# Buffers rounded to 512 bytes, and four small pads that shift the weight buffers and some inputs against the others

## The chip, the cores and the metric

The program runs on one core of a Trainium2 chip. The metric is device time of one execution in microseconds (us). A core has a matrix engine (TensorE, PE in the tables, with PEld for its weight loads), a vector engine (VectorE, DVE), a scalar engine (ScalarE, ACT), GpSimd (POOL) and a queue engine (SyncE, SP). Operands lie in an on-chip memory of 128 partitions; every buffer below has the same start address in each partition. All addresses and sizes in this document are bytes within one partition.

## The reference

A block attention whose output feeds a gated linear unit, both in 32-bit floats:

```
scores = q @ k^T / sqrt(64)                 # 8 batches, 8 heads, 576 positions, 64 per head
heads 0-3: keep keys with 0 <= row - key < 32
heads 4-7: keep keys <= row in the same class modulo 32
attn   = softmax(scores) @ v
x      = attn, heads side by side           # 4608 tokens x 512
y      = (sigmoid(x @ w_gate) * (x @ w_val)) @ w_out     # 512 -> 1536 -> 512
```

Nearly all arithmetic is in the last line: three products with 512 x 1536 or 1536 x 512 matrices.

## The kernel before

Every float operand of the large products is split into a high part and a low remainder, and one product is done as three matmuls in the one-pass float format (fp32r): high x high, high x low, low x high. `three` issues them in this order for weights `wh, wl` and inputs `xh, xl`: (wh, xh), (wh, xl), (wl, xh). In each matmul a 128 x 128 block of the first operand is loaded into the engine as weights (one LDWEIGHTS), and 512 columns of the second stream through it (the moving operand).

The tokens are handled in a first part (the first batch, 512 tokens) and then four superblocks of up to two batches. The first part forms `g` and `v` (gate and value) from inputs named `x0_0` to `x0_3` (buffers `t0` to `t3`; the profile strips digits and prints `x`) and weights `w` (buffers `w0` to `w3`), then output sums `o`. In a superblock, two batches and two feature chunks are combined in a seven-product scheme (P1 to P7): inputs `x0` to `x6`, each with a high and a low part, and weights `mix` with seven parts of high and low. For five of the inputs, high and low are buffers of their own (`x0h`, `x0l`, ...); `x4` and `x5` are one buffer each with both halves, and the profile prints both as `x` (rows `x,mix`). Each of the seven products of one of the six pairs of chunks is 6 matmuls into a gate bank `g` and then 6 into a value bank `v`, in the order P1, P5, P6, P2, P7, P3, P4, whose inputs by the table `X_OF` are x0, x1, x3, x2, x5, x4, x6 (the very first pair alone does P2 ahead of P6).

The second half of superblocks 2 to 4 is the product with `w_out`, by parts as well; its operands share one buffer called `stage`: moving columns and weights lie in the same buffer. Superblock 1 does it plainly, with moving `wo` and weights `hs` in neighbouring buffers of the ring.

`mix`, `stage`, `wo` and `hs` all take the next of the ring of four buffers `w0` to `w3` in turn (`next_of_ring`). Between the large products stand short runs of small matmuls of the attention of later batches (scores `s`, transposes `t`, weighted values `x<-pt,vv`).

The order on every engine is written out by hand in the strings `ORDERS` and recorded as it stands (`manual_schedule`). Buffers come from one pool, `keep`: a tag gets its place when it is first asked for, directly behind the tag before it (rounded up to 32 bytes), and keeps it. So the sizes and the order of first requests fix every address. `flat` is the helper that asks for nearly all of them; `LINE = 32` floats (128 bytes) is its rounding.

Of the kernel before, what the change touches and what calls it, by code (L numbers as in the profile page):

```python
# [18 lines left out]
DM, DF = 512, 1536  # L19
NT = B * S  # L20
P = 128
LINE = 32
STRIDE = 32
QB = 64
LB = 32
# [223 lines left out]
def attention_then_glu(ctx, tc, qk_l, qk_s, v_l, v_s, w_all, consts, out):  # L249
    nc = tc.nc  # L250
    pool = ctx.enter_context(tc.tile_pool(name="keep", bufs=1))
# [4 lines left out]
    of_start = ExitStack()  # L256
    start_ps = of_start.enter_context(tc.tile_pool(name="start_ps", bufs=1, space=bass.MemoryType.PSUM))

    def flat(tag, n, name, dtype=F32):

        spare = -n % LINE
        return pool.tile([P, n + spare], dtype, tag=tag, name=name)[:, :n] if spare else pool.tile([P, n], dtype, tag=tag, name=name)

    cst = pool.tile([P, SL * KL + GS + P], F32, tag="cst", name="cst")
    some = slice(0, P), slice(P, P + SL * KL), slice(P + SL * KL, P + SL * KL + GS)
    ident, mask_l, mask_s = (cst[:, part] for part in some)
    mask_l = mask_l.rearrange("p (j n) -> p j n", j=1)
# [13 lines left out]
    def first_inputs():  # L281
        for c in range(NC):
            both = flat(f"t{c}", 2 * TB, f"x0_{c}", F32R)
            xs0["h", c], xs0["l", c] = both[:, :TB], both[:, TB:]
# [4 lines left out]
    def batch_tiles(b):  # L289
        if b not in rest:  # L290
            rest[b] = flat("xr", NC * REST, f"xr{b}")
            if b:
                raw[b] = flat("raw_a" if b % 2 else "raw_b", NC * TB, f"raw{b}")
# [1004 lines left out]
```

## Time and profile before

| | |
|---|---|
| median of 2 runs | 914.35 us (913.95 and 914.75) |
| the profiled execution's own time | 913.73 us |
| its span, first to last instruction | 911.9 us |
| PE busy, share of the span | 904.4 us, 99% |
| DVE, ACT, POOL busy | 615.3, 458.4, 288.2 us |
| granted TensorE clock over the span | 0.999 of full speed |
| chain of waits that ended last | PE 97%, DVE 2% |

The rounded shares of the page say that PE works all the time, but not how densely: a matmul's printed length is modelled and overlaps the next one's. The timeline is better for that: it prints the start of each merged run of matmuls and the count, so the distance between two starts divided by the count is the time that one matmul takes in the stream.

### The profile page before, as it was taken

What the parts mean: (1) busy time and instruction counts of PE and PEld (TensorE: products, weight loads), DVE (VectorE), ACT (ScalarE), POOL (GpSimd) and SP (SyncE); (2) the same over time, 40 slices, a digit from 0 to 9 for tenths busy, and PEclk for the clock granted to TensorE, in tenths of its full rate; (3) what the DMA queues carried; (4) which work ended last, traced back from release to release, by engine and by line L of the source; (5) the groups of instructions that cost most, each with busy time, mean ns of one, the idle gap of its engine ahead of it and who ended that gap; (6) DMA issues with size and microseconds to landing.
All of it is one profiled execution on the core that took longest, in us unless ns stands there. A gap on an engine that the chain in (4) does not pass through costs nothing.

```text
span 911.9 us, 18834 instructions
## 1 busy us (share of the span) xinstructions
PE 904.4 (99%) x7612; PEld 735.3 (81%) x7612; DVE 615.3 (67%) x967; ACT 458.4 (50%) x839; POOL 288.2 (32%) x234
## 2 busy tenths in 40 slices
PE   9999999999999999999999999999999999999997
PEld 8788888888888778888878888888888888888887
DVE  6887767887646788878678987322699853223955
ACT  5776887585433343646446544322546443233451
POOL 3244336644210252522025451000415620001165
PEclk9999999999999999999999999999999999999999
DMA  8888872865526789999664689558346796651566
GB/s 326 301 313 312 294 263 92 346 283 236 238 88 222 247 276 341 383 354 336 262 219 144 203 266 313 207 220 323 135 131 202 226 296 247 234 224 46 162 206 165
DMA packets 91623, 220.76 MB, mean 242 GB/s; under 512 B 35856, under 2 KB 50832, under 8 KB 84368
## 3 DMA queue, kind: packets, MB, share of 16 engines
q1 hardware_dynamic: 87216, 218.50, 67.7%
q10 hardware_dynamic: 4320, 1.05, 0.5%
q8 instruction: 60, 0.98, 0.4%
q14 instruction: 27, 0.22, 0.1%
HBM read 171.29 MB, written 48.23 MB: 241 GB/s over the span
## 4 chain that ended last, share of the span: by engine, by line
PE 97%; DVE 2%; issue 0%; ACT 0%; POOL 0%; DVEq 0%; POOLq 0%
PE g__2137 L610 15%; PE v__2139 L610 15%; PE v__2141 L610 10%; PE g__2140 L610 10%; PE g__2136 L610 10%; PE v__2138 L610 10%; PE x L471 4%; PE o L660 4%; PE g L610 3%; PE v L610 3%; PE s L368 3%; PE g__2140 L660 2%; PE v__2141 L660 2%; PE g__2136 L660 1%; PE v__2138 L660 1%; PE g__2137 L660 1%
## 5 line engine op out<-in xcount | busy, mean ns | idle before, releaser
L929 POOL TENSOR_TENSOR stage<-h,stage 128x512 fp32r<-128x512 f32 x50 | 75.5, 1529 | 165.9 <-ACT stage L927 144.7
L927 ACT CAST stage<-h 128x512 fp32r<-128x512 f32 x126 | 73.2, 620 | 73.6 <-issue 21.2
L443 DVE STREAM_TRANSPOSE pt<-sb 32x320 f32<-32x320 f32 (+1 forms) x160 | 85.8, 536 | 17.8 <-PE x L471 14.1
L796 DVE TENSOR_TENSOR s<-g__2137,gp 128x512 f32<-128x512 f32 x24 | 16.6, 690 | 79.1 <-PE g__2137 L610 58.5
L929 DVE TENSOR_TENSOR stage<-h,stage 128x512 fp32r<-128x512 f32 x76 | 61.7, 830 | 9.6 <-ACT stage L927 5.9
L798 ACT ACTIVATE s<-s 128x512 f32<-128x512 f32 x48 | 30.3, 633 | 54.7 <-DVE s L796 54.6
L797 DVE TENSOR_TENSOR h<-s 128x512 f32<-128x512 f32 x48 | 36.2, 761 | 23.6 <-ACT s L798 22.8
L798 ACT ACTIVATE s<-g__2137 128x512 f32<-128x512 f32 x24 | 14.3, 595 | 59.3 <-PE g__2137 L610 59.3
L610 PE MATMUL g__2137<-stage 128*128 128x512 f32 (+1 forms) x162 | 39.4, 380 | 0.0
L610 PE MATMUL v__2139<-stage 128*128 128x512 f32 (+1 forms) x162 | 39.3, 379 | 0.0
L610 PE MATMUL v__2141<-x,mix 128*128 128x512 f32 x144 | 37.7, 396 | 0.0
L610 PE MATMUL g__2140<-x,mix 128*128 128x512 f32 x144 | 37.7, 396 | 0.0
L610 PE MATMUL v__2139<-x,mix 128*128 128x512 f32 x144 | 37.6, 396 | 0.0
L610 PE MATMUL g__2137<-x,mix 128*128 128x512 f32 x144 | 37.5, 395 | 0.0
L847 POOL TENSOR_TENSOR hs<-h,hs 128x512 fp32r<-128x512 f32 x12 | 15.4, 1294 | 65.3 <-ACT hs L845 65.3
L471 PEld LDWEIGHTS x<-pt,vv 64*64 64x64 f32 (+1 forms) x1592 | 28.5, 134 | 8.9 <-issue 8.1
L610 PE MATMUL g<-x,w 128*128 128x512 f32 x132 | 34.1, 402 | 0.4 <-DVE x L506 0.4
L402 POOL TENSOR_TENSOR sb<-sb,mx 128x648 f32<-128x648 f32 (+1 forms) x9 | 12.8, 1420 | 68.4 <-DVE mx L394 68.2
L610 PE MATMUL v__2139<-x3h,mix 128*128 128x512 f32 x96 | 34.1, 395 | 0.0
L610 PE MATMUL v__2141<-x1h,mix 128*128 128x512 f32 x96 | 34.0, 395 | 0.0
L610 PE MATMUL g__2136<-x2h,mix 128*128 128x512 f32 x96 | 33.9, 394 | 0.0
L610 PE MATMUL g__2137<-x6h,mix 128*128 128x512 f32 x96 | 33.9, 394 | 0.0
(280 smaller groups left out, 2487.7 us busy)
## 6 DMA issues: line engine op xcount, KB each, us to landing
mix<-mix SPq DMA_DIRECT2D x36, 1024.0 KB, 8.8
mix<-mix SPq DMA_DIRECT2D x36, 768.0 KB, 6.5
mix<-mix SPq DMA_DIRECT2D x12, 1792.0 KB, 6.2
stage<-sums_out SPq DMA_DIRECT2D x72, 256.0 KB, 3.6
stage<-outer SPq DMA_DIRECT2D x54, 256.0 KB, 3.2
wo<-outer SPq DMA_DIRECT2D x8, 1536.0 KB, 6.8
vv<-in_v_l SPq DMA_DIRECT2D x16, 640.0 KB, 6.4
qk<-in_qk_l SPq DMA_DIRECT2D x16, 592.0 KB, 6.3
```

What stands on the lines that cost most here:

```text
L368: nc.tensor.matmul(sc[g * m : (g + 1) * m, j * BANK + s * kk : j * BANK + (s + 1) * kk], qk[d, q0 : q0 + m], qk[d, k0 : k0 + kk], start=no ...
L402: engine.tensor_tensor(prob, src, by_row, op=ALU.subtract)
L443: nc.vector.transpose(dst[to : to + LB, :, col : col + LB], src[rows : rows + LB, :, h * LB : (h + 1) * LB])
L471: nc.tensor.matmul(xp[j * D : (j + 1) * D, r * BANK + (u * per + g) * m : r * BANK + (u * per + g + 1) * m], v[rows, (u * per + g) * P + j ...
L610: nc.tensor.matmul(o, w, x, start=first and n == 0, stop=last and n == len(todo) - 1, skip_group_check=onto)
L660: nc.tensor.matmul(o, a[:, i * P : (i + 1) * P], b, start=first and n == 0, stop=last and n == 2)
L796: add = lambda to, x, y: nc.vector.tensor_tensor(to, x, y, op=ALU.add)
L797: mul = lambda to, x, y: nc.vector.tensor_tensor(to, x, y, op=ALU.mult)
L798: sig = lambda to, x: nc.scalar.activation(to, x, AF.Sigmoid)
L847: engine.tensor_tensor(hl, src, hh.bitcast(F32), op=ALU.subtract)
L927: nc.scalar.copy(h, src)
L929: engine.tensor_tensor(l, src, h.bitcast(F32), op=ALU.subtract)
```

## The change

`flat` now rounds a buffer to `ROW = 128` floats (512 bytes) if it has at least that many, and leaves smaller ones as they are. The two small buffers for row maxima (`mx`, `mx2`) are asked for first, right behind the constants. And at the first request of `w0`, `w1`, `w2` and `x6h`, a pad of 8, 8, 16 and 24 floats (32, 32, 64 and 96 bytes) is put ahead.

```
-LINE = 32
+ROW = 128
+APART = {'w0': 8, 'w1': 8, 'w2': 16, 'x6h': 24}
...
+    seen = set()
+
     def flat(tag, n, name, dtype=F32):

-        spare = -n % LINE
+        if tag in APART and tag not in seen:
+            pool.tile([P, APART[tag]], dtype, tag=tag + "_apart", name=tag + "_apart")
+        seen.add(tag)
+        spare = -n % ROW if n >= ROW else 0
...
+    for tag in ("mx", "mx2"):
+        flat(tag, 16, tag)
```

On each of the five engines the built program holds the same instructions in the same order with the same waits as before; only addresses differ. Start of each buffer modulo 256, from the built programs (before: modulo 512 in brackets):

| buffers, in the order of their addresses | before | after |
|---|---|---|
| t0 to t3 (x0_0 to x0_3 of the first part) | 96 (96) | 224 |
| x1h, x3h, x5, x4, x0l | 96 (352) | 224 |
| x0h | 224 (480) | 224 |
| w0 | 224 (480) | 0 |
| x1l, x2h, x3l | 224 (480) | 0 |
| w1 | 224 (480) | 32 |
| w2 | 224 (480) | 96 |
| x6h, x2l, x6l | 224 (480) | 192 |
| w3, and all that follow | 224 (480) | 192 |

Before, every one of these starts is 96 modulo 128. Within a buffer, weights begin at multiples of 512 bytes and moving operands of 512 columns at multiples of 2048, so these remainders hold for every large matmul. The last buffer ends 352 bytes later than before.

Below, the **distance** of a matmul is the difference between the start of its moving operand and the start of the weights that are loaded for the matmul behind it, modulo 256 and the shorter way round, so 0 to 128. Counted in program order over the 3455 matmuls of 512 columns that have another behind them (small matmuls between left out):

| matmuls of 512 columns | before: 0 / 128 | after: 0 / 32 / 64 / 96 / 128 |
|---|---|---|
| first part, g and v (288) | 0 / 288 | 0 / 148 / 70 / 0 / 70 |
| x4 and x5 with mix (576) | 0 / 576 | 0 / 288 / 144 / 0 / 144 |
| x0 with mix (288) | 192 / 96 | 0 / 144 / 72 / 0 / 72 |
| x1 and x3 with mix (576) | 192 / 384 | 48 / 240 / 144 / 48 / 96 |
| x2 with mix (288) | 288 / 0 | 72 / 48 / 72 / 96 / 0 |
| x6 with mix (288) | 288 / 0 | 72 / 0 / 72 / 144 / 0 |
| o of the first part (144) | 144 / 0 | 33 / 0 / 35 / 76 / 0 |
| wo with hs (288) | 288 / 0 | 0 / 140 / 8 / 140 / 0 |
| stage (719) | 719 / 0 | 660 / 15 / 29 / 15 / 0 |
| all (3455) | 2111 / 1344 | 885 / 1023 / 646 / 519 / 382 |

## Rows read from the trace of the kernel before

**Rows 1.** The page: the span, busy time by engine, the granted clock, the last chain.

```profile
span 911.9 us, 18834 instructions
...
PE 904.4 (99%) x7612; PEld 735.3 (81%) x7612; DVE 615.3 (67%) x967; ACT 458.4 (50%) x839; POOL 288.2 (32%) x234
...
PEclk9999999999999999999999999999999999999999
...
PE 97%; DVE 2%; issue 0%; ACT 0%; POOL 0%; DVEq 0%; POOLq 0%
```

**Rows 2.** Waits of PE: who waited for whom, us in total, times, longest.

```profile
PE zeros_out L651 <- POOL zeros L642: 1.0, 1, 1.0
PE g L649 <- issue: 0.6, 1, 0.6
PE early L610 <- DVE early_base L991: 0.6, 1, 0.6
PE t L430 <- DVE first_x L422: 0.5, 1, 0.5
PE g L610 <- DVE x L506: 0.4, 1, 0.4
```

**Rows 3.** Timeline of PE, stage matmuls: start, length, line, out<-in, weights, moving, count.

```profile
532.83 1.52 PE L610 MATMUL g__2140<-stage 128*128 128x512 f32 x6
...
543.71 1.52 PE L610 MATMUL g__2137<-stage 128*128 128x512 f32 x6
```

**Rows 4.** Timeline of PE: inputs x2, x5, x4, x6 of one pair.

```profile
205.85 0.40 PE L610 MATMUL g__2136<-x2h,mix 128*128 128x512 f32 x1
...
208.62 1.55 PE L610 MATMUL g__2137<-x,mix 128*128 128x512 f32 x6
210.01 1.56 PE L610 MATMUL v__2139<-x,mix 128*128 128x512 f32 x6
211.41 1.56 PE L610 MATMUL g__2140<-x,mix 128*128 128x512 f32 x6
212.81 1.56 PE L610 MATMUL v__2141<-x,mix 128*128 128x512 f32 x6
214.21 0.39 PE L610 MATMUL g__2137<-x6h,mix 128*128 128x512 f32 x1
```

**Rows 5.** Timeline of PE, the first part's value sums and what follows.

```profile
112.01 2.96 PE L610 MATMUL v<-x,w 128*128 128x512 f32 x12
114.81 0.45 PE L354 MATMUL s<-rounded 128*128 128x320 f32 x2
```

**Rows 6.** Timeline of PE: x6, then x0, x1 and x3, up to x2.

```profile
420.13 0.39 PE L610 MATMUL g__2137<-x6h,mix 128*128 128x512 f32 x1
...
422.86 0.39 PE L610 MATMUL g__2136<-x0h,mix 128*128 128x512 f32 x1
...
431.10 0.40 PE L610 MATMUL g__2136<-x2h,mix 128*128 128x512 f32 x1
```

**Rows 7.** Timeline of PE: x6 right behind x4, four matmuls.

```profile
440.62 0.40 PE L610 MATMUL g__2137<-x6h,mix 128*128 128x512 f32 x1
...
441.56 0.39 PE L610 MATMUL g__2137<-x6l,mix 128*128 128x512 f32 x1
```

**Rows 8.** Timeline of PE: stage matmuls of 256 columns near the end.

```profile
898.03 0.88 PE L610 MATMUL early<-stage 128*128 128x256 f32 x6
...
900.91 1.60 PE L610 MATMUL early<-stage 128*128 128x256 f32 x12
```

**Rows 9.** Groups by line and form: x4 and x5 with mix; busy us, mean ns.

```profile
L610 PE MATMUL v__2141<-x,mix 128*128 128x512 f32 x144 | 37.7, 396 | 0.0
L610 PE MATMUL g__2140<-x,mix 128*128 128x512 f32 x144 | 37.7, 396 | 0.0
L610 PE MATMUL v__2139<-x,mix 128*128 128x512 f32 x144 | 37.6, 396 | 0.0
L610 PE MATMUL g__2137<-x,mix 128*128 128x512 f32 x144 | 37.5, 395 | 0.0
```

## The prediction

> **What bounds the kernel now.** I read the page first, then PE's waits, then the timeline of PE. The page has PE busy for 99% of a span of 911.9 us at full clock, and the chain that ended last is PE for 97% of it [rows 1]. The list of PE's waits holds five entries of 3.1 us together [rows 2]. So no other engine, no queue and no transfer sets the end: the time is the sum of what each matmul takes in PE's stream, and a change that moves no instruction can reach the end only through the length of single matmuls. The reader is to see next that this length isn't the same everywhere although the shapes are. Between the starts of two stage runs lie 48 matmuls (eight runs of 6) in 543.71 - 532.83 = 10.88 us, 226.7 ns each [rows 3]. The 24 matmuls on x5 and x4 take 214.21 - 208.62 = 5.59 us, 232.9 ns each [rows 4], and the 12 of the first part 114.81 - 112.01 = 2.80 us, 233.3 ns each [rows 5]. All are 128x512 of the same type with one weight load each.
>
> What tells them apart is in the table of distances: stage has distance 0 throughout; x4, x5 and the first part have 128 throughout. The mixed inputs lie between: x0, x1 and x3, where one or two of three matmuls have distance 128, take 431.10 - 422.86 = 8.24 us for 36, 228.9 ns each [rows 6]. Distance is not all: x2 and x6 have distance 0 throughout, and x2 takes (208.62 - 205.85)/12 = 230.8 ns in front of x5 [rows 4], x6 between 227.5 ns over 12 [rows 6] and 235.0 ns over its first four right behind x4 [rows 7]. It reads like two streams that fall into step when their starts agree, and that need some matmuls to find the step again after a product in which they don't.
>
> The runs of 256 columns give the fixed part: 24 matmuls in 900.91 - 898.03 = 2.88 us, 120.0 ns each [rows 8]. From 256 to 512 columns that is 106.7 ns more, or 2.4 GHz, one column a cycle; 120.0 - 106.7 leaves 13.3 ns per matmul at distance 0, whatever its length, and 20.0 ns at distance 128.
>
> **The change part by part.** *What the mechanism is worth before.* Over 226.7 ns: x4 and x5, 576 (the four rows of 144 [rows 9]) x 6.2 ns = 3.6 us; first part 288 x 6.6 = 1.9; x0, x1, x3, 864 x 2.2 = 1.9; x2 288 x 4.1 = 1.2; x6 288 x 0.8 = 0.2. Together 8.8 us, 1% of the profiled 913.73 us. If all distances went to 0, this is what would be won.
>
> *What the new distances cost.* After the change 382 matmuls have distance 128 in place of 1344, but 885 have 0 in place of 2111; 2188 have 32, 64 or 96, which no row of before shows: every start there is 96 modulo 128. The nearest rows are the two ends, 0 ns at distance 0 [rows 3] and 6.7 ns at 128 [rows 5]. If only 128 costs, the bill is 382 x 6.7 = 2.6 us, 6.2 less than now. If the price grows evenly with distance, it is 6.7/128 x (1023 x 32 + 646 x 64 + 519 x 96 + 382 x 128 = 172800) = 9.0 us, 0.2 more than now. Below nothing, or above 6.7 ns, can't be excluded by rows either; these are the two rivals below. I take the middle of the two readings, 5.8 us, 3.0 less than now: distance 32 (1023 matmuls) lies nearer the cheap end and 96 (519) nearer the dear one, while the row of x6 warns that streams out of step cost something also where the start agrees.
>
> *The pads, the larger rounding, the early request of the maxima's buffers.* They add no instruction and no wait. Vector, scalar and GpSimd work on shifted addresses too; if that made some of them a few ns longer, PE's 3.1 us of waits [rows 2] show how seldom it waits for them, and DVE with 67% busy [rows 1] is the fullest of the others. I count 0; if the cover failed, the wait on the sum `early_base` near the end (0.6 us [rows 2]) would be the first to grow. The transfers have the same sizes and order, and PE waits for none: 0. The small matmuls between the large runs keep their distances within one buffer, or work from buffers that were shifted alike: 0.
>
> *Sum.* 913.7 - 3.0 = 910.7 us by the profiled execution, which lies 0.6 us under the median of 914.35; so 911 us for the median. The forecast's own range, with the two readings as ends, is 908 to 915.
>
> *A rule against the change.* The stage and x5/x4 rows differ by 6.2 ns at the same shape [rows 3, 4], which the distance of two reads explains. The Trainium skill, SBUF — State Buffer, section Who interferes with whom, says that TensorE has two independent read ports, one for the moving operand and one for weight loads, and that PE never waits on anyone. By that rule no start address could cost anything and the change would be worth 0; the trace doesn't agree as far as the two rows go together with the distances, but it doesn't prove the cause.
>
> **Rivals.** *Addresses are not the cause (0.10).* The 6.2 ns could come from what else goes on in those stretches. For it: x2 and x6 are slow at distance 0. Against it: runs at distance 0 come back to 226.7 ns in all ring buffers, and the first part and x4, x5, far apart in the program, agree within 0.4 ns. Time: unchanged, 914.
>
> *The step is lost (0.17), slower.* With remainders 0, 32, 96, 192 and 224 modulo 256 in play, hardly two products in a row have the same distance, and inside x1, x2, x3 it changes from matmul to matmul. If streams find their step only where distance is 0, PE runs as it does right behind x4: 235.0 ns [rows 7], 8.3 over the floor. On the 2570 matmuls at distances other than 0 that is 21.3 us in place of 8.8: 913.7 + 12.5 + 0.6 = 927. For it: x2 and x6 show that being out of step costs up to that. Against: x0, x1 and x3 alternate between distances 0 and 128 and pay only 2.2 ns. It decides against the change from an average of 8.8 us / 2570 = 3.4 ns on these matmuls, 230.1 ns each.
>
> *The fixed part falls (0.15), faster.* The 13.3 ns at distance 0 [rows 3, 8] may be a collision itself: two reads that start at the same remainder, the price that shifting by less than 128 bytes would take away. Bounds for what is left of it are 0 and 13.3; at half, the 2570 matmuls win 2570 x 6.7 = 17.1 us and the 8.8 us besides: 913.7 - 25.9 + 0.6 = 888. For it: 13.3 ns is constant over two lengths, as a collision with a weight load of fixed size would be. Against: the stage runs, at distance 0 from end to end, are the densest that I found, and a fixed exchange of weights would look the same. The Trainium skill, TensorE: Matmul & The Clock Gate, section "Wait — 56ns, not 53.3ns?", gives 215.7 ns from start to start for bf16 matmuls of 512 columns; if these came to that, the estimate would be 877; no run of this type shows it.
>
> **How the numbers follow.** Forecast 0.58 (908 to 915), addresses without effect 0.10 (914), step lost 0.17 (914 to 927, all of it at the upper end only if every product suffers), fixed part falls 0.15 (about 905 if a quarter of the matmuls gain, 888 if all). Predicted: 911. The range 898 to 924 holds the first two cases, most of the third and the milder half of the fourth; about 0.15 is left out. Two per cent, about what a measurement of this kernel tells from no change, is 18.3 us: under 896 or above 932.6. The first takes the stronger half of the fixed-part case, 0.08. The second needs more than every product at the worst row, 0.03. Within: 0.89.
>
> **What the new profile would show.** Stage still at 226.7 ns, since it lies in one buffer; if stage changes, the remainder itself counts and not the distance. x5 and x4 no longer alike in all pairs: at 233 ns where the weights lie in w2, and nearer 227 to 230 with w0, w1 and w3. The first part in the same way by its ring buffer. x2 and x6, at distance 0 until now, slightly slower. PE's waits still about 3 us. Wrong would be the forecast if x5 and x4 with w0 and w3 (distance 32) stay at 233 or go above, or if any run of 512 columns falls below 226.

## The result: 922.58 us, slower by 0.9%

The changed kernel took 922.58 us as median of 2 runs (922.54 and 922.62) beside 914.35 us before: ratio 1.0091, 95% interval 1.0071 to 1.0111. The profiled execution took 922.54 us with a span of 920.7 us, 8.8 more than before. This is the page of the changed kernel; the shares hardly differ from [rows 1], and PE was busy for 8.0 us more with as many instructions.

```profile
span 920.7 us, 18834 instructions
...
PE 912.4 (99%) x7612; PEld 735.6 (80%) x7612; DVE 615.5 (67%) x967; ACT 458.6 (50%) x839; POOL 287.9 (31%) x234
...
PEclk9999999999999999999999999999999999999999
...
PE 97%; DVE 1%; issue 1%; ACT 0%; POOL 0%; ACTq 0%; POOLq 0%; DVEq 0%
```

The waits of PE in the changed kernel come to 4.0 us in six entries, where [rows 2] had 3.1. So the loss isn't waiting; it has to lie in the lengths of matmuls.

```profile
PE zeros_out L660 <- POOL zeros L651: 1.0, 1, 1.0
PE g__2143 L619 <- ACT early_base L1022: 0.9, 1, 0.9
PE g L658 <- issue: 0.6, 1, 0.6
PE early L619 <- DVE early_base L1000: 0.6, 1, 0.6
PE t L439 <- DVE first_x L431: 0.5, 1, 0.5
PE g L619 <- DVE x L515: 0.4, 1, 0.4
```

The timeline of PE in the changed kernel, x2, x5, x4 and x6 of one pair up to x0 (start, length, line, out<-in, weights, moving, count):

```profile
206.51 0.39 PE L619 MATMUL g__2142<-x2h,mix 128*128 128x512 f32 x1
...
209.28 1.56 PE L619 MATMUL g__2143<-x,mix 128*128 128x512 f32 x6
210.69 1.56 PE L619 MATMUL v__2145<-x,mix 128*128 128x512 f32 x6
212.08 1.56 PE L619 MATMUL g__2146<-x,mix 128*128 128x512 f32 x6
213.48 1.56 PE L619 MATMUL v__2147<-x,mix 128*128 128x512 f32 x6
214.88 0.40 PE L619 MATMUL g__2143<-x6h,mix 128*128 128x512 f32 x1
...
217.69 0.39 PE L619 MATMUL g__2142<-x0h,mix 128*128 128x512 f32 x1
```

x5 and x4 take 214.88 - 209.28 = 5.60 us for 24 matmuls, 233.3 ns each, against 232.9 in [rows 4]: nothing was won. x6 takes (217.69 - 214.88)/12 = 234.2 ns against 227.5 in [rows 6]. The same view further on, x0, x1 and x3 up to x2:

```profile
425.74 0.40 PE L619 MATMUL g__2142<-x0h,mix 128*128 128x512 f32 x1
...
434.09 0.39 PE L619 MATMUL g__2142<-x2h,mix 128*128 128x512 f32 x1
```

36 matmuls in 8.35 us, 231.9 ns each, against 228.9 [rows 6]. And the stage matmuls, eight runs of 6 from the first row to the last:

```profile
536.69 1.55 PE L619 MATMUL g__2146<-stage 128*128 128x512 f32 x6
538.08 1.52 PE L619 MATMUL v__2147<-stage 128*128 128x512 f32 x6
539.43 1.54 PE L619 MATMUL g__2146<-stage 128*128 128x512 f32 x6
540.82 1.55 PE L619 MATMUL v__2147<-stage 128*128 128x512 f32 x6
...
547.71 1.56 PE L619 MATMUL g__2143<-stage 128*128 128x512 f32 x6
```

48 in 11.02 us, 229.6 ns each, against 226.7 [rows 3], although moving operand and weights lie in one buffer. The printed length of a run shows it too: 1.52 to 1.56 us here, 1.52 in [rows 3].

For the whole program I took the time from the start of every 512-column matmul to the start of the next, left out gaps of 300 ns and more (waits, small matmuls between), and averaged by class; some 3,315 gaps are left in each kernel. The difference is the mean's change times the intervals that are left in the class (249 of 288 in the first part, 702 of 719 of stage):

| class (matmuls) | before, ns | after, ns | difference, us |
|---|---|---|---|
| first part, g and v (288) | 232.6 | 232.7 | 0.0 |
| x0 (288) | 229.1 | 232.4 | +0.95 |
| x1, x3 (576) | 229.1 | 232.3 | +1.8 |
| x2 (288) | 229.9 | 232.1 | +0.6 |
| x4, x5 (576) | 232.9 | 232.7 | -0.2 |
| x6 (288) | 228.6 | 232.6 | +1.15 |
| o of the first part (144) | 229.4 | 231.5 | +0.3 |
| wo with hs (288) | 228.3 | 233.2 | +1.3 |
| stage (719) | 227.0 | 230.1 | +2.2 |

Together 8.2 of the span's 8.8 us. The slow classes stayed slow; of the others all but stage came near them, and stage took half the way.

### The profile page after: what moved, and what is told of

Read it like the earlier page. It is cut to its first block, busy times and chain, and to the rows that moved or that the text cites. A ratio compares the mean times of both kernels' runs of the same rounds, so it can differ in the third digit from the quotient of the medians.

```text
span 920.7 us, 18834 instructions
## 1 busy us (share of the span) xinstructions
PE 912.4 (99%) x7612; PEld 735.6 (80%) x7612; DVE 615.5 (67%) x967; ACT 458.6 (50%) x839; POOL 287.9 (31%) x234
## 4 chain that ended last, share of the span: by engine, by line
PE 97%; DVE 1%; issue 1%; ACT 0%; POOL 0%; ACTq 0%; POOLq 0%; DVEq 0%
PE g__2143 L619 15%; PE v__2145 L619 15%; PE g__2142 L619 10%; PE v__2144 L619 10%; PE v__2147 L619 10%; PE g__2146 L619 10%; PE o L669 4%; PE x L480 4%; PE g L619 3%; PE v L619 3%; PE s L377 3%; PE g__2146 L669 2%; PE v__2147 L669 2%; PE g__2142 L669 1%; PE g__2143 L669 1%; PE v__2145 L669 1%
## 5 line engine op out<-in xcount | busy, mean ns | idle before, releaser
L619 PEld LDWEIGHTS g__2143<-stage 128*128 128x128 f32 x162 | 29.0, 188 | 7.2 <-ACT early_base L1022 1.1
L619 PE MATMUL v__2144<-x0h,mix 128*128 128x512 f32 x96 | 34.2, 397 | 0.0
```

What stands on the lines that cost most here:

```text
L619: nc.tensor.matmul(o, w, x, start=first and n == 0, stop=last and n == len(todo) - 1, skip_group_check=onto)
```

## Experiments

**Theory**: a matmul streams at 226.7 ns only if its moving operand and the weights loaded beside it start at the same remainder modulo 256; any other distance costs some 6 ns at once, not in proportion. Below, "in step" means streaming at 226.7 ns; the step theory of the expectations is this one. **Rivals**: the price grows with distance (the prediction); the remainder of the moving operand alone, or an absolute remainder, counts; addresses are not the cause. All ten kernels hold the same instructions, order and waits as the kernel before on every engine, so a difference between two of them is one of addresses; the granted clock was 0.999 or 1.000 of full speed in every profiled execution. Diffs are against the changed kernel unless said otherwise.

### The rounding alone

```
-APART = {'w0': 8, 'w1': 8, 'w2': 16, 'x6h': 24}
+APART = {}
```

> The change without its four pads: every large buffer starts at 224 modulo 512, all distances are 0. Step theory (226.7 ns only where moving operand and weights agree and have agreed for some matmuls; about 6 ns more at any other distance): x0 to x6, first part, wo and stage all at about 227 ns; 913.7 - 8.4 = 905 us. Graded theory (the price grows with distance up to 6.7 ns at 128): the same, 905. Theory that the larger rounding or the early request of the small buffers costs the 8 us: 920 to 923.

Measured: 907.05 us (4 runs, 906.4 to 907.58) beside 914.58, ratio 0.9914 [0.9892, 0.9935]; span 905.5 us. Its page, and its timeline for x5, x4 and the first x6:

```profile
span 905.5 us, 18834 instructions
...
PE 897.2 (99%) x7612; PEld 735.9 (81%) x7612; DVE 615.7 (68%) x967; ACT 458.4 (51%) x839; POOL 287.3 (32%) x234
```

```profile
207.63 1.52 PE L619 MATMUL g__2139<-x,mix 128*128 128x512 f32 x6
208.99 1.52 PE L619 MATMUL v__2141<-x,mix 128*128 128x512 f32 x6
210.35 1.52 PE L619 MATMUL g__2142<-x,mix 128*128 128x512 f32 x6
211.71 1.52 PE L619 MATMUL v__2143<-x,mix 128*128 128x512 f32 x6
213.07 0.39 PE L619 MATMUL g__2139<-x6h,mix 128*128 128x512 f32 x1
```

1.36 us from run to run, 226.7 ns a matmul: x5 and x4 now stream as stage does in [rows 3]. The means of x0 to x6 are 226.9 to 227.3 ns, stage is 227.0. The large matmuls together fall from 760.7 to 753.2 us, 7.5 less, as much as the median. So addresses are the cause, and the pads are what makes the change slow.

Three classes stay above 227 ns although all starts agree: the first part at 228.4, wo at 228.0, o at 227.4. What they share is that short runs of small matmuls interrupt them often. A stage run behind such an interruption shows the effect:

```profile
543.99 1.04 PE L377 MATMUL s<-qk 64*32 64x64 f32 x80
544.95 1.67 PE L619 MATMUL g__2139<-stage 128*128 128x512 f32 x6
546.46 1.55 PE L619 MATMUL v__2141<-stage 128*128 128x512 f32 x6
547.85 0.39 PE L619 MATMUL g__2138<-x0h,mix 128*128 128x512 f32 x1
```

The second six take 1.39 us, as x5 and x4 did before. Over this kernel the first eight matmuls behind an interruption (a first interval of 300 ns and more left out) take 229.8 ns on average, and all later ones 226.7 to 226.8 in every class. So an interruption, too, puts the stream out of step for some matmuls; whether by the pause or by the small matmuls' own starts isn't shown.

### The weight ring 32, 128 and 256 bytes off

```
-APART = {'w0': 8, 'w1': 8, 'w2': 16, 'x6h': 24}
+APART = {}
+RING_APART = 8        # 32 and 64 in the two others
...
+    pool.tile([P, RING_APART], F32, tag="ahead", name="ahead")
+    for f in range(4):
+        flat(f"w{f}", THREE * 2 * DM, f"place{f}", F32R)
+    pool.tile([P, ROW - RING_APART], F32, tag="behind", name="behind")
```

All inputs have one remainder, the whole ring another; stage, wo and hs lie wholly in the ring.

> All four ring buffers at one remainder, 32 bytes from that of all other buffers (asked for together, a pad of 32 bytes ahead and 480 behind). Every matmul with an input outside the ring (mix, first part, o: 2448) has distance 32 throughout; stage and wo have 0. Step theory: mix at about 233 ns, stage and wo at 227; 904.2 + 2448 x 6.4 = 920 us. Graded theory, in which the changing remainders made the loss: a quarter of 6.7 ns, mix at 228.4; 904.2 + 1.1 + 4.1 = 909 us.

> As the run before, with the ring at 128 bytes from the rest: mix, first part and o at distance 128 with the moving operand at 224 modulo 256; stage and wo at distance 0 with the moving operand at 96. If the distance counts (step and graded theory alike): mix 233, stage 227; 920 us. If the remainder of the moving operand itself counts (224 good, 96 bad, which the rows of before allow too): mix 227, stage and wo 233; 904.2 + 1008 x 6.4 + 1 = 912 us.

> As the two runs before, with the ring at 256 bytes from the rest. If distance counts modulo 256: no difference to the run without pads, mix 227, 905 us. If modulo 512 or more: mix 233, 920 us.

Measured: 920.33 us with 32 bytes, 920.23 with 128, 907.43 with 256 (one run each, before 914.58). The kernel with 32 bytes, x5 to x6, then stage:

```profile
209.71 1.56 PE L624 MATMUL g__2145<-x,mix 128*128 128x512 f32 x6
...
215.31 0.40 PE L624 MATMUL g__2145<-x6h,mix 128*128 128x512 f32 x1
...
536.08 1.52 PE L624 MATMUL g__2148<-stage 128*128 128x512 f32 x6
...
546.96 1.52 PE L624 MATMUL g__2145<-stage 128*128 128x512 f32 x6
```

The kernel with 128 bytes, x5 to x6:

```profile
209.81 1.56 PE L624 MATMUL g__2145<-x,mix 128*128 128x512 f32 x6
...
215.38 0.40 PE L624 MATMUL g__2145<-x6h,mix 128*128 128x512 f32 x1
```

At 32 bytes 24 matmuls take 5.60 us, 233.3 ns each; at 128 bytes 5.57 us, 232.1. Stage in the first of them is at 10.88/48 = 226.7 ns. The means of x0 to x6 are 233.2 to 233.3 ns at distance 32, 232.6 to 233.0 at 128, 226.9 to 227.3 at 256. The price is a step: a quarter of the distance costs the whole of it, rather more. Starts 256 bytes apart are as good as starts 0 apart. And it isn't the remainder of the moving operand: the inputs have the remainder that they have with the rounding alone; only the ring's is another.

### One pad only

```
-APART = {'w0': 8, 'w1': 8, 'w2': 16, 'x6h': 24}
+APART = {'w0': 8}
```

All from `w0` on moves by 32 bytes against the inputs ahead of it: nearly the pattern of the kernel before, with 32 bytes in place of 128. Only x0 differs: both its halves now lie ahead of `w0`, so all its matmuls are off, where a third was.

> The first of the four pads alone: w0 and all buffers behind it lie at 0 modulo 256, those ahead of it at 224. x4, x5, x0 and the first part have distance 32 throughout, x1 and x3 in two of three matmuls, x2, x6, o, wo and stage 0. Step theory: x4, x5, x0 and the first part at 233 ns, x1 and x3 between 229 (as before the change, with 128 in two of three) and 233, stage at 227; 907 + 5.5 + 1.4 + 1.2 to 3.6 + 1 = 916 to 919 us. Graded theory is out by the second run; if 32 cost only through a change of remainder, 910.

Measured: 918.17 us in one run (before 914.5). x2 and x6, still at distance 0, are at 229.8 and 228.5 ns as before; x1 and x3, two thirds of whose matmuls are off as before, went from 229.1 to 233.1, and x0, now off throughout, to 233.4. The kernel takes 3.7 us more than the one before, of which 864 x 4.1 ns = 3.5 us are theirs, and 11.1 us more than the rounding alone, from which it differs by this one pad. In x1 and x3 the matmuls at distance 0 between the others take 231.0 to 231.3 ns (before: 226.6 to 227.7): mixed with matmuls at distance 0, those off by 32 bytes are dearer than those off by 128.

### Everything at remainder 0

```
-APART = {'w0': 8, 'w1': 8, 'w2': 16, 'x6h': 24}
+APART = {}
...
+    pool.tile([P, 72], F32, tag="ahead", name="ahead")
```

> No pads among the buffers, one pad of 288 bytes ahead of all of them: every large buffer starts at 0 modulo 512 in place of 224. If only the agreement counts: as without pads, mix 227, 907 us. If the remainder itself counts, another time, up to 920.

Measured: 906.08 us in one run (before 914.5); x0 to x6 at 226.8 to 227.2 ns. The absolute remainder doesn't count.

### One input 16 bytes off

```
-APART = {'w0': 8, 'w1': 8, 'w2': 16, 'x6h': 24}
+APART = {}
...
+        if tag == "x5":
+            return pool.tile([P, n + ROW], dtype, tag=tag, name=name)[:, 4 : 4 + n]
```

> No pads, but x5 begins 16 bytes into its buffer: its 288 matmuls have distance 16, all others 0. If the step is at 16 bytes or less: x5 at 233 ns and x4 behind it some ns up; 907 + 1.8 + 0.7 = 909.5 us. If the two streams agree by blocks of 32 bytes or more that 224 and 240 share: x5 at 227, 907.

Measured: 909.39 us in one run (before 914.5), 2.3 over the rounding alone. x5, then x4, which is at distance 0, up to x6:

```profile
207.50 1.55 PE L621 MATMUL g__2139<-x,mix 128*128 128x512 f32 x6
208.89 1.55 PE L621 MATMUL v__2141<-x,mix 128*128 128x512 f32 x6
210.28 1.55 PE L621 MATMUL g__2142<-x,mix 128*128 128x512 f32 x6
211.67 1.52 PE L621 MATMUL v__2143<-x,mix 128*128 128x512 f32 x6
213.03 0.39 PE L621 MATMUL g__2139<-x6h,mix 128*128 128x512 f32 x1
```

x5 takes 1.39 us a run, 231.7 ns a matmul (231.5 over the program, where I expected 233). The first six of x4, all in agreement, take 1.39 us again; only the second six are at 1.36. So a matmul that agrees isn't yet in step: here it takes six of them to get back to 226.7 ns. No other input moved (226.9 to 227.3).

### The old rounding with one number doubled

Against the kernel before, which has neither pads nor the early request of `mx` and `mx2`:

```
-LINE = 32
+LINE = 64
```

> The kernel before with one number changed: LINE = 64, so that buffers are multiples of 256 bytes and all start at 96 modulo 256. Step theory with a period of 256: mix 227, 907 us, ratio 0.991. If multiples of 512 are wanted, or 96 is a bad remainder: 914 to 920.

Measured: 907.08 us (4 runs, 906.39 to 908.43) beside 914.5, ratio 0.9922 [0.9905, 0.9938]. Rounding to 256 bytes is all that is needed: in the kernel before some buffers are an odd number of 128 bytes long, and each moves all that follow by half a period.

### Ring buffers that agree within, but not with each other

Stage lost 2.2 us though it agrees with itself. Its runs take `w0` to `w3` in turn, at remainders 0, 32, 96 and 192; the change of remainder from run to run is the suspect. Two kernels put a pad behind each ring buffer, 32 floats, or 8 and 56 in turn, so that the common remainder jumps by 128 or by 32 bytes:

```
-APART = {'w0': 8, 'w1': 8, 'w2': 16, 'x6h': 24}
+APART = {}
...
+    for f in range(4):
+        flat(f"w{f}", THREE * 2 * DM, f"place{f}", F32R)
+        pool.tile([P, 32], F32, tag=f"behind{f}", name=f"behind{f}")   # or (8, 56)[f % 2]
```

> No pads among the other buffers; w0 and w2 agree with them modulo 256, w1 and w3 lie 128 away. Stage has distance 0 inside each buffer, and its remainder changes from buffer to buffer, every 12 matmuls. If a change of remainder costs some matmuls out of step although each buffer agrees with itself (the reading of stage after the change): stage at 229 to 231 ns, 702 x 3 = 2.1 us. If stage was slowed by its new remainders as such, 0, 32, 96 and 192: stage at 227 here. Mix has its gate products and its value products at different distances, six matmuls each: 230 to 233 ns; in all 907 + 2 + 8 to 14 = 917 to 923 us.

> As the run before, with w1 and w3 at 32 bytes from the rest in place of 128. The run before found two slow matmuls per change of buffer in stage, 227.9 ns on average, where the change has ten and 230.1. If the size of the jump in remainder decides how long stage is out of step: here about ten slow matmuls in at least one direction, stage at 229 to 230 ns. If any jump costs two matmuls and the change's 230.1 has another cause: 227.9. Gate and value products at distances 32 and 0 in turn: mix at 230 to 233; in all 917 to 922 us.

Measured: 917.54 us (before 914.2) with jumps of 128 bytes, 918.76 (before 914.18) with 32, one run each. Mix came as expected, 230.5 to 230.9 ns. `wo` and `hs`, whose buffers are neighbours in the ring and no longer agree, went from 228.0 to 233.1 and 233.5: the distance again. Stage with jumps of 128:

```profile
535.21 1.55 PE L622 MATMUL g__2150<-stage 128*128 128x512 f32 x6
...
546.16 1.52 PE L622 MATMUL g__2147<-stage 128*128 128x512 f32 x6
```

And with jumps of 32:

```profile
536.04 1.52 PE L622 MATMUL g__2150<-stage 128*128 128x512 f32 x6
...
547.03 1.55 PE L622 MATMUL g__2147<-stage 128*128 128x512 f32 x6
```

48 matmuls in 10.95 us (228.1 ns) and in 10.99 us (229.0); over the program 227.9 and 229.5 ns. The second hit the expectation, the first missed it: after a jump of 128 bytes only about two matmuls are slow. The single starts of the 12 matmuls on one buffer show how it goes (ns to the next start, in the order of the program):

```
before, no jump                   227 227 226 ...
rounding alone, interrupted       236 229 232 231 227 226 ...
after, 192 to 0                   228 230 233 236 224 231 236 228 232 231 227 235
after, 0 to 32                    230 224 231 236 228 233 230 227 227 226 227 226
jumps of 32, one way              230 236 229 232 231 227 226 ...
jumps of 32, the other way        230 224 231 236 228 233 231 226 ...
jumps of 128                      232 231 227 ...
x5 at distance 32                 235 232 235 232 ...
```

The same jump gives nearly the same sequence each time, and all come back by way of 232 or 233 and then 231 or 230 to 227 and 226; a 235 at a row's end belongs to the next jump. The second row is a stage run behind small matmuls, its first, longer interval left out: the way back is the same. This settles the stage term: every jump of the common remainder costs a few slow matmuls until the stream is in step again, and on ring buffers of 12 matmuls that can be nearly all of them.

## Why the prediction failed

The forecast was 911 us, faster; the kernel became slower, to 922.58. That the range of 898 to 924 still holds this owes to the rival on the slower side, not to the sum.

**The price of the distances, the failed step.** "I take the middle of the two readings" made 32, 64 and 96 bytes cheaper than 128. There is no middle: 16 bytes cost 4.6 ns (231.5 against 226.9), and 32 cost 6.3 and 128 cost 5.8 ns in kernels where one distance holds for all inputs. No kernel has 64 or 96 throughout, but classes of the changed kernel have them for six matmuls at a time, between others that are off: x4 and x5 at 64 take 233.1 and 233.2 ns, x6 at 64 and 96 takes 233.3 and 233.4. The two readings were both drawn through one point, 128; nothing before spoke for a price that grows. With the step, 2570 matmuls at distances other than 0 cost 2570 x 5.8 = 14.9 us over the floor in place of the 5.8 forecast. The starts in the trace say the same: over 226.7 ns, the matmuls off distance 0 cost 14.5 us (7.0 before), stage at distance 0 costs 2.3 (0.2) and all others at distance 0 cost 0.8 (2.3). That is 17.7 us against 9.5, the 8.2 of the table.

**Stage counted as unchanged, the second failed step.** It has 2.2 of the 8.2 us. [Rows 4, 7] had shown x2 and x6 slow at distance 0, and I read this as out of step behind a product at distance 128. That was right; that a change of the common remainder throws the step as well was named ("if stage changes, the remainder itself counts and not the distance") but had no term. Both count: the remainder's change for some matmuls, the distance for all.

**What the mechanism was worth before** was right in kind and near in size: 8.8 us forecast if all distances were 0; the rounding alone won 7.5. The first part was the term most over: 1.9 us forecast, but it only falls from 232.6 to 228.4 ns, 288 x 4.2 = 1.2 us, because interruptions hold it above the floor. x2 was 0.3 over, from one stretch at 230.8 ns against a mean of 229.9.

**The step is lost**, the rival on the slower side, is what happened. Its signs came as written: x5 and x4 with `w0` and `w3` (distance 32) stayed at 232.5 to 233.2 ns, w1 (64) is no cheaper at 233.1 and 233.2, and w2 (128), where I expected the worst, is the cheapest at 230.9 and 232.3. Its 927 us took 235.0 ns for every matmul off distance 0, from the four behind x4 [rows 7]; they take 232 to 233. It left out stage.

**Addresses are not the cause** fell: the rounding alone and the ring 32 bytes off differ in addresses alone, and by 13.3 us. The Trainium skill, SBUF — State Buffer, section Who interferes with whom, has PE with two independent read ports, one for the moving operand and one for weight loads, and never waiting on anyone. As far as "independent" means that the start of one stream can't cost the other time, 226.7 against 233.3 ns at the same shape, by start addresses alone, disagrees, and the measurement decides. That PE waits on no other engine for its reads is not tested by any run here.

**The fixed part falls** fell too: no class mean in any kernel is below 226.8 ns, and every distance other than 0 made them longer.

**The costs put at nothing** held: DVE, ACT and POOL are busy within 0.3 us of [rows 1], and PE's waits grew by 0.9 us. The small matmuls' term can't be far from 0: the 512-column matmuls account for all but 0.6 of the span's 8.8 us.

## What to carry to other kernels

Where PE is the bound, compare starts of the same shape along its timeline, not busy shares: 6 ns of 227 show only there. For 32-bit matmuls in the one-pass format, let moving operands and weights start at one common remainder modulo 256 bytes in all buffers that follow each other. Rounding every buffer to 256 bytes did it here, for 0.8% and with one number changed, since inside the buffers operands begin at multiples of 512 anyway; no pad is needed. When a cost is known at two ends only, a step fits them as well as a line: price the step, too, before choosing the middle.

## What the runs showed that I had not expected

- A matmul of 512 columns took 226.7 ns in step and 231.5 to 233.4 out of step, whether the starts were 16, 32 or 128 bytes apart; 256 apart was as good as 0. This is with 128x128 weights in the one-pass format; no other type was tried.
- Being in step has a memory: after a change of the common remainder, two matmuls (128 bytes) to about ten (192 to 0) ran slow, in the same sequence each time. An interruption by small matmuls does the same with all starts in agreement: 229.8 ns over the first eight, 226.7 after.
- With two of three matmuls off, 128 bytes cost 229.1 ns on average and 32 bytes 233.1: in mixed company the farther distance is the cheaper one.

Left open: what in the chip makes the two starts matter to each other, why the way back into step takes up to ten matmuls, and what the 13.3 ns are that each matmul takes beyond its columns even in step; no kernel here changed the latter. Nor is it settled whether a matmul's own weights count or those loaded for the one behind it: where stage changes its buffer, the last interval on the old buffer is already long at jumps of 32 and 128 bytes (235 and 232 ns), but not at jumps of 64 and 96 (226 and 228).
